# Swapped operand of the scores: second turn on TensorE, or a transfer from SBUF to SBUF

## Chip, cores and metric

One core of a Trainium2 chip. The time is the device time of the program in microseconds (us). Engines: TensorE (PE; its weight loads are PEld), VectorE (DVE), ScalarE (ACT), GpSimd (POOL), SyncE (SP), which issues all transfers of this kernel.

## What is computed

Attention that keeps 32 scores of each row, then two layers of expert networks. Cut to what matters:

```python
# q, k, v: (2, 8, 576, 64) float32; 2 batches, 8 heads
scores = (1 / sqrt(64)) * q @ k.transpose(0, 1, 3, 2)
kth = the 32nd largest score of each row
attn = softmax(where(scores >= kth, scores, -1e9))
x = (attn @ v) -> (1152, 512)
# 4 experts: out += p[:, e] * (relu(x @ w1[e]) @ w2[e]);  w1: (4, 512, 1024), w2: (4, 1024, 512)
# then a gated layer: ((x @ w_a) * (x @ w_b)) @ w_out;    w_a, w_b: (512, 1536), w_out: (1536, 512)
```

Which scores are kept depends on small differences, so most products are made nearly in float32.

## The kernel before

**Products.** Most operands are split into a high part, rounded to the fp32r format, and a low part, the rest. For the scores, k is turned so that its 64 high values and 64 low values of a row stand on 128 partitions, [high; low]. q is turned into two operands: [high; low], which gives high x high + low x low, and [low; high], which gives the two mixed products. The two matmuls add up in PSUM (`scores`, L765; `lh` counts the two operands).

**Tiles and groups.** The 1152 rows of q are nine tiles: eight of 128 rows, and one, MIX, with the last 64 rows of both batches. They are worked through in four groups of 1, 2, 3 and 3 tiles (`GROUPS`), MIX being the last tile of group 3. A group goes through four pairs of heads; `start_pair` (L679) prepares a pair: loads q (`qraws`), splits it (`split2`, L597), turns it and evicts it. Then each tile of the pair is a step: scores of both heads, their eviction (L794), four rounds of top-k on DVE (`MAX8` L815, `MATCH_REPLACE8` L823), mask and softmax on ACT and POOL (L846, L850, L854), scaling (L865), the turning of the probabilities (L538) and their product with v. When a group's four pairs are done, its experts' matmuls can run on PE between the steps of the next groups; the experts of group 3 and the gated layer stand behind the attention.

**Preparing q (L708 to L751).** Per head j, ACT writes the high part twice (blocks 0 and 2 of three) and DVE (first step) or POOL writes the low part in block 1. A turn then transposes blocks 0 and 1 and blocks 1 and 2 of each tile into one PSUM tile:

```python
                for i in range(T):
                    for lh in range(2):
                        tr(p[:, i, lh], sqv()[:, j, i, lh:lh + 2].rearrange("p a d -> p (a d)"), identr)
```

This is a turn of 2 T transposes per head, evicted by ACT into `qts` (L743, for the very first one by DVE, L739). For MIX the columns of each batch are copied into `qm` (L749), which holds zeros elsewhere; there is one `qm`, so its next contents wait for the last scores that read it (`qm_read`).

**PSUM.** `atts` are two double banks that take turns: scores, turns of k, q and probabilities all pass through them.

**Order.** Every operation is given to `Plan` with its engine, an estimated duration, a key (the lower, the sooner) and what it waits for. `best` simulates 42 orders, with transfers that land some time after their issue, and keeps the one with the lowest mean over three reruns. The engines then execute that order strictly, SP its transfers too (`load`, L514; all show as L517). All matmuls have line L535, all transposes L538.

Of the kernel before, what the change touches and what calls it, by code (L numbers as in the profile page):

```python
# [21 lines left out]
MIX = "mix"  # L22
# [354 lines left out]
def body(tc, q, k, v, probs, w1, w2, wa, wb, wo, out):  # L377
# [73 lines left out]
    qspls = big.slots("qspl", 1, 2 * 3 * 3 * D)  # L451
    qts = big.slots("qt", 2, 3 * 256)
# [100 lines left out]
    def last_rows(x, b):  # L553
        return x[b, :, MAIN:S].rearrange("h p d -> p h d")
# [123 lines left out]

    def start_pair(c, h2, n):  # L679
# [22 lines left out]
        sqv = lambda: sq.ap[:, 0:2 * T * 3 * D].rearrange("p (h t a d) -> p h t a d", h=2, t=T, a=3)  # L702
# [8 lines left out]
        sp = {0: [], 1: []}  # L711
        for j in range(2):
            sp[j] += split2(lambda j=j: sqv()[:, j, 0:m], lambda j=j: rqv()[:, j], m, key + 0.03 + (0.004 * j if n == 0 else 0), lds, [rq, sq], eng)
            if m < T:
                if not qrem_done:
                    for b in range(B):
                        qrem_done.append(load(lambda b=b: qrem[b * REM:(b + 1) * REM], lambda b=b: last_rows(q, b), key - 2, (), (), 131072, since=60e3))
                sp[j] += split2(lambda j=j: sqv()[:, j, m:T], lambda j=j: qrem[:, h + j].unsqueeze(1), 1, key + 0.03, qrem_done, [sq], eng)
        pair.q, pair.qd = {}, {}
        for j in range(2):  # L720
            at, qt = ms.tile() if n == 0 else atts.tile(key + 0.04), qts.tile(n)
            if n == 0:
                pv = lambda at=at: at.ap[:, 0:256].rearrange("p (t l n) -> p t l n", l=2, n=128)
            else:
                pv = lambda at=at: at.ap.rearrange("p b (t l n) -> p (b t) l n", l=2, n=128)

            def turn(j=j, pv=pv):
                p = pv().bitcast(F32R)
                for i in range(T):
                    for lh in range(2):  # L730
                        tr(p[:, i, lh], sqv()[:, j, i, lh:lh + 2].rearrange("p a d -> p (a d)"), identr)

            o = tensor(2 * T * TURN_R, turn, key + (0.025 if n == 0 and j == 0 else 0.04), sp[j] + [ready], [at, sq])
            qtv = lambda qt=qt: qt.ap.rearrange("p (t l n) -> p t l n", l=2, n=128)
            pair.q[j] = qt
            if n == 0 and j == 0:

# [728 lines left out]
```

## Time and profile before

| | |
|---|---|
| median of 3 runs | 829.12 us (829.0 to 829.53) |
| profiled execution | 828.9 us; its span, first to last instruction, 827.1 us |
| PE busy / DVE / ACT / POOL | 795.7 / 738.8 / 537.4 / 351.7 us |
| mean granted TensorE clock | 0.988 |
| moved by DMA | 129.68 MB, mean 157 GB/s |

Busy time is the time in which an engine has an instruction in work; matmuls overlap, so a busy PE is not one at its peak. A stretch of the span is read by the engine that is full in it and by what the others wait for there; idle time of an engine that nobody waits for costs nothing. The chain that ended last is followed back from the last instruction.

### The profile page before, as it was taken

What the parts mean: (1) busy time and instruction counts of PE and PEld (TensorE: products, weight loads), DVE (VectorE), ACT (ScalarE), POOL (GpSimd) and SP (SyncE); (2) the same over time, 40 slices, a digit from 0 to 9 for tenths busy, and PEclk for the clock granted to TensorE, in tenths of its full rate; (3) what the DMA queues carried; (4) which work ended last, traced back from release to release, by engine and by line L of the source; (5) the groups of instructions that cost most, each with busy time, mean ns of one, the idle gap of its engine ahead of it and who ended that gap; (6) DMA issues with size and microseconds to landing.
All of it is one profiled execution on the core that took longest, in us unless ns stands there. A gap on an engine that the chain in (4) does not pass through costs nothing.

```text
span 827.1 us, 14615 instructions
## 1 busy us (share of the span) xinstructions
PE 795.7 (96%) x5285; PEld 711.2 (86%) x5285; DVE 738.8 (89%) x1447; ACT 537.4 (65%) x953; POOL 351.7 (43%) x333
## 2 busy tenths in 40 slices
PE   7589999999999999999999999999999999999997
PEld 6477777798888789899989899989998989899996
DVE  7999999999899999999985899988867899997654
ACT  6878887999898989997765666766534633341110
POOL 3524333797978867755320201222213334432220
PEclk9789999999999999999999999999999999999999
DMA  6839976755466252433234646989320412221013
GB/s 218 257 102 339 310 230 218 235 166 176 155 195 200 81 193 85 159 103 103 77 128 159 205 146 220 331 269 324 112 94 4 151 52 103 76 78 52 1 52 114
DMA packets 91416, 129.68 MB, mean 157 GB/s; under 512 B 10832, under 2 KB 67152, under 8 KB 89808
## 3 DMA queue, kind: packets, MB, share of 16 engines
q1 hardware_dynamic: 91344, 128.75, 47.4%
q8 instruction: 41, 0.67, 0.3%
q14 instruction: 31, 0.25, 0.1%
HBM read 115.36 MB, written 13.37 MB: 156 GB/s over the span
## 4 chain that ended last, share of the span: by engine, by line
PE 65%; DVE 17%; ACT 10%; POOL 3%; issue 3%; DMA 1%; SPq 0%; POOLq 0%; DVEq 0%; ACTq 0%
PE ps L535 63%; DVE low L815 8%; DVE low L823 6%; PE ps L538 3%; POOL mid L981 2%; ACT mid L980 2%; ACT low L854 1%; ACT low L846 1%; ACT lowa L794 1%; ACT low L865 1%; ACT lowa L923 1%; DMA raw<-in_moe_w_dram 1%; POOL low L850 1%; ACT mid L1050 1%; DVE mid L1054 0%
## 5 line engine op out<-in xcount | busy, mean ns | idle before, releaser
L535 PE MATMUL ps<-mid 128*128 128x512 f32 x1092 | 278.7, 394 | 1.4 <-POOL mid L981 1.3
L535 PEld LDWEIGHTS ps<-mid 128*128 128x128 f32 x1092 | 198.6, 188 | 35.1 <-POOL mid L981 2.2
L535 PE MATMUL ps<-xs,mid 128*128 128x384 f32 (+1 forms) x1152 | 204.8, 321 | 2.6 <-DVE mid L1054 2.1
L535 PEld LDWEIGHTS ps<-xs,mid 128*128 128x128 f32 x1152 | 184.3, 189 | 11.9 <-DVE mid L1054 2.9
L815 DVE MAX8 low<-low 128x8 f32<-128x576 f32 x216 | 154.5, 748 | 0.1
L1271 POOL TENSOR_TENSOR low<-low 128x512 int32<-128x512 int32 x36 | 51.3, 1424 | 169.7 <-DVE low L1268 110.4
L981 POOL TENSOR_TENSOR mid<-raw,mid 128x1024 fp32r<-128x1024 f32 x48 | 115.0, 2409 | 7.4 <-ACT mid L980 5.5
L850 POOL TENSOR_TENSOR low<-lowa,low 128x576 f32<-128x576 f32 x70 | 99.2, 1438 | 36.6 <-ACT low L846 36.5
L980 ACT ACTIVATE mid<-raw 128x1024 fp32r<-128x1024 f32 x96 | 102.1, 1072 | 16.6 <-PE ps L535 12.0
L823 DVE MATCH_REPLACE8 low<-low 128x576 f32<-128x576 f32 x144 | 106.2, 743 | 0.0
L535 PE MATMUL ps<-xs,big 128*128 128x320 f32 (+1 forms) x576 | 87.7, 296 | 0.1
L535 PEld LDWEIGHTS ps<-xs,big 128*128 128x128 f32 x576 | 81.3, 190 | 2.5 <-DVE low L1360 0.3
L981 DVE TENSOR_TENSOR mid<-raw,mid 128x1024 fp32r<-128x1024 f32 x48 | 63.1, 1314 | 6.7 <-ACT mid L980 6.6
L535 PE MATMUL ps<-lowa_again,big 128*128 128x320 f32 (+1 forms) x432 | 67.0, 297 | 1.2 <-ACT rest L1369 0.8
L1050 ACT ACTIVATE mid<-ps 128x384 fp32r<-128x384 f32 (+1 forms) x96 | 44.3, 464 | 35.2 <-PE ps L535 32.5
L535 PEld LDWEIGHTS ps<-lowa_again,big 128*128 128x128 f32 x432 | 61.5, 189 | 3.8 <-ACT rest L1369 1.1
L865 ACT ACTIVATE low<-low 128x576 f32<-128x576 f32 x70 | 52.1, 790 | 16.3 <-DVE low L862 16.2
L538 PE MATMUL ps<-identr,low 128*128 128x128 f32 x360 | 52.5, 282 | 8.8 <-ACT low L865 7.8
L1054 DVE SCALAR_TENSOR_TENSOR mid<-ps,mid 128x384 fp32r<-128x384 f32 (+1 forms) x96 | 48.3, 505 | 12.7 <-ACT mid L1050 12.3
L846 ACT ACTIVATE low<-lowa,low 128x576 f32<-128x576 f32 x70 | 53.7, 786 | 7.3 <-POOL low L840 7.3
L538 PEld LDWEIGHTS ps<-identr,low 128*128 128x128 f32 x360 | 42.7, 144 | 17.8 <-ACT low L865 11.3
L794 ACT ACTIVATE lowa<-ps 128x576 f32<-128x576 f32 x72 | 47.4, 663 | 15.4 <-POOL low L850 11.3
(119 smaller groups left out, 1221.9 us busy)
## 6 DMA issues: line engine op xcount, KB each, us to landing
raw<-in_moe_w_dram SPq DMA_DIRECT2D x122, 512.0 KB, 4.0
big<-kscr SPq DMA_DIRECT2D x20, 576.0 KB, 5.4
low<-in_v_dram SPq DMA_DIRECT2D x24, 256.0 KB, 3.6
low<-in_moe_w_b_dram SPq DMA_DIRECT2D x12, 512.0 KB, 3.7
low<-in_moe_w_a_dram SPq DMA_DIRECT2D x12, 512.0 KB, 4.1
low<-in_moe_w_out_dram SPq DMA_DIRECT2D x12, 512.0 KB, 4.4
wscr<-big SPq DMA_DIRECT2D x6, 1024.0 KB, 7.1
mid<-wscr SPq DMA_DIRECT2D x6, 1024.0 KB, 4.8
```

Of the source, the lines that this page charges most:

```text
L535: nc.tensor.matmul(out, l, r, **kw)
L538: nc.tensor.transpose(out, a, i)
L794: S, lambda: nc.scalar.activation(s.ap.rearrange("p (c n) -> p c n", c=2), at.ap[:, :, 0:HALF], AF.Copy),
L815: 62 + 1.04 * width, lambda at=at, cs=cs: nc.vector.max(m8v()[:, x, cs], at()), key + 0.02 * r, [done],
L823: lambda at=at, cs=cs: nc.vector.match_replace(out=src[1](), in_to_replace=m8v()[:, x, cs], in_values=at(), imm_value=LOW),
L846: S, lambda x=x, s=s: nc.scalar.activation(ev(x), s.ap, AF.Relu, bias=endv()[:, x, 1:2], scale=-STEEP),
L850: pool_(S), lambda x=x, s=s: nc.gpsimd.tensor_tensor(ev(x), s.ap, ev(x), op=ALU.subtract), ks, [a], [s, ep]
L865: S, lambda x=x: nc.scalar.activation(ev(x), ev(x), AF.Copy, scale=sums.ap[:, x:x + 1]),
L980: hi = scalar(1024, lambda: nc.scalar.activation(u.ap[:, 0:1024], r.ap, AF.Copy), 500 + s, [ld], [u, r], sbuf=True)
L981: sub = lambda eng: eng.tensor_tensor(u.ap[:, 1024:2048], r.ap, u.ap[:, 0:1024], op=ALU.subtract)
L1050: n, lambda h=h, p=p: nc.scalar.activation(h.ap[:, 0:n], p.ap[:, 0:n], AF.Relu), -1000, [o], [h, p]
L1271: return gpsimd(pool_(512), lambda: nc.gpsimd.tensor_tensor(t().bitcast(I32), fold(c.ap.bitcast(I32)), fold(lowv().bitcast(I32)), op=ALU.a ...
```

## The change

Group 0 keeps its two turns per head (`first_queries`). In groups 1 to 3 (`queries`) q is split into a high and a low part once, for both heads in one instruction per engine; one turn for both heads makes [high; low] only, and one ACT instruction evicts it into `qa`. Two transfers then copy partitions 64 to 127 of `qa` to partitions 0 to 63 of `qb` and the other way round, which makes [low; high]. There are two `qa` and one `qb`. For MIX two ACT copies fill the first half of `qm`, and two transfers make the swapped half. A pair's scores wait for both transfers.

```diff
@@
     big.at = 2048
     kspls = big.slots("kspl", 1, 2 * M4 * 2 * D)
     bts = big.slots("bt", 4, 2 * S)
-    qspls = big.slots("qspl", 1, 2 * 3 * 3 * D)
-    qts = big.slots("qt", 2, 3 * 256)
+    qspls = big.slots("qspl", 1, 2 * 3 * 2 * D)
+    qas = big.slots("qa", 2, 2 * 3 * 128)
+    qbs = big.slots("qb", 1, 2 * 3 * 128)
@@
 
     qm_read = [[], []]
 
+    def first_queries(pair, n, key, eng, rqv, tiles, lds):
+
+        rq, sq = tiles
+        qa = qas.tile(n)
+        sqv = lambda: sq.ap[:, 0:2 * 3 * D].rearrange("p (h t a d) -> p h t a d", h=2, t=1, a=3)
+        pair.qd, pair.q = {}, [qa]
+        pair.qv = lambda j, i, lh: qa.ap[:, (2 * j + lh) * 128:(2 * j + lh + 1) * 128]
+        for j in range(2):
+            sp = split2(lambda j=j: sqv()[:, j], lambda j=j: rqv()[:, j], 1, key + 0.03 + (0.004 * j if n == 0 else 0), lds, tiles, eng)
+            at = ms.tile() if n == 0 else atts.tile(key + 0.04)
+            pv = (lambda at=at: at.ap[:, 0:256]) if n == 0 else (lambda at=at: at.ap[:, 0, 0:256])
+
+            def turn(j=j, pv=pv):
+                for lh in range(2):
+                    tr(pv().bitcast(F32R)[:, lh * 128:(lh + 1) * 128], sqv()[:, j, 0, lh:lh + 2].rearrange("p a d -> p (a d)"), identr)
+
+            o = tensor(2 * TURN_R, turn, key + (0.025 if n == 0 and j == 0 else 0.04), sp + [ready], [at, sq])
+            qv = lambda j=j: qa.ap[:, j * 256:(j + 1) * 256]
+            if n == 0 and j == 0:
+                pair.qd[j] = [vector(dve(256), lambda pv=pv, qv=qv: nc.vector.tensor_copy(qv(), pv()), -901.5, [o], [at, qa])]
+            else:
+                pair.qd[j] = [scalar(256, lambda pv=pv, qv=qv: nc.scalar.activation(qv(), pv(), AF.Copy), -901.5 + j, [o], [at, qa])]
+
+    def queries(pair, n, key, eng, rqv, tiles, lds):
+
+        rq, sq = tiles
+        T, h, m = pair.T, pair.h, len([t for t in pair.tiles if t != MIX])
+        qa, qb, at = qas.tile(n), qbs.tile(n), atts.tile(key + 0.04)
+        sqv = lambda: sq.ap[:, 0:2 * T * 2 * D].rearrange("p (h t a d) -> p h t a d", h=2, t=T, a=2)
+        sp = split(lambda: sqv()[:, :, 0:m, 0], lambda: sqv()[:, :, 0:m, 1], rqv, 2 * m * D, key + 0.03, lds, tiles, eng)
+        if m < T:
+            if not qrem_done:
+                for b in range(B):
+                    qrem_done.append(load(lambda b=b: qrem[b * REM:(b + 1) * REM], lambda b=b: last_rows(q, b), key - 2, (), (), 131072, since=60e3))
+            sp += split(lambda: sqv()[:, :, m, 0], lambda: sqv()[:, :, m, 1], lambda: qrem[:, h:h + 2], 2 * D, key + 0.03, qrem_done, [sq], eng)
+
+        def turn():
+            p = at.ap.bitcast(F32R)
+            for j in range(2):
+                for i in range(T):
+                    tr(p[:, j, i * 128:(i + 1) * 128], sqv()[:, j, i].rearrange("p a d -> p (a d)"), identr)
+
+        o = tensor(2 * T * TURN_R, turn, key + 0.04, sp + [ready], [at, sq])
+        w = m * 128
+        av = lambda: qa.ap[:, 0:2 * w].rearrange("p (j n) -> p j n", j=2)
+        bv = lambda: qb.ap[:, 0:2 * w].rearrange("p (j n) -> p j n", j=2)
+        e = scalar(2 * w, lambda: nc.scalar.activation(av(), at.ap[:, :, 0:w], AF.Copy), -901, [o], [at, qa])
+        got = [e] + [
+            load(lambda r=r: bv()[r * 64:(r + 1) * 64].bitcast(F32), lambda r=r: av()[(1 - r) * 64:(2 - r) * 64].bitcast(F32), -500, [e], [qa, qb], 512 * w)
+            for r in range(2)
+        ]
+        pair.qd, pair.q = {0: got, 1: got}, [qa, qb]
+        pair.qv = lambda j, i, lh: (bv() if lh else av())[:, j, i * 128:(i + 1) * 128]
+        if m < T:
+            es_ = [
+                scalar(
+                    2 * REM, lambda b=b: nc.scalar.activation(
+                        qm[:, :, b, 0, b * REM:(b + 1) * REM], at.ap[:, :, w + b * REM:w + (b + 1) * REM], AF.Copy
+                    ), -900, [o] + qm_read[0] + qm_read[1], [at],
+                ) for b in range(B)
+            ]
+            qm_read[:] = [], []
+            pair.md = es_ + [
+                load(lambda r=r: qm[r * 64:(r + 1) * 64, :, :, 1].bitcast(F32), lambda r=r: qm[(1 - r) * 64:(2 - r) * 64, :, :, 0].bitcast(F32), -400, es_, (), 1 << 17)
+                for r in range(2)
+            ]
+
     def start_pair(c, h2, n):
 
         pair = Pair()
@@
         m = len(norm)
         rq, sq = qraws.tile(key), qspls.tile(key)
         rqv = lambda: rq.ap[:, 0:2 * m * D].rearrange("p (h m d) -> p h m d", h=2, m=m)
-        sqv = lambda: sq.ap[:, 0:2 * T * 3 * D].rearrange("p (h t a d) -> p h t a d", h=2, t=T, a=3)
...
-        sp = {0: [], 1: []}
-        for j in range(2):
-            sp[j] += split2(lambda j=j: sqv()[:, j, 0:m], lambda j=j: rqv()[:, j], m, key + 0.03 + (0.004 * j if n == 0 else 0), lds, [rq, sq], eng)
-            if m < T:
-                if not qrem_done:
-                    for b in range(B):
-                        qrem_done.append(load(lambda b=b: qrem[b * REM:(b + 1) * REM], lambda b=b: last_rows(q, b), key - 2, (), (), 131072, since=60e3))
-                sp[j] += split2(lambda j=j: sqv()[:, j, m:T], lambda j=j: qrem[:, h + j].unsqueeze(1), 1, key + 0.03, qrem_done, [sq], eng)
-        pair.q, pair.qd = {}, {}
-        for j in range(2):
-            at, qt = ms.tile() if n == 0 else atts.tile(key + 0.04), qts.tile(n)
-            if n == 0:
-                pv = lambda at=at: at.ap[:, 0:256].rearrange("p (t l n) -> p t l n", l=2, n=128)
-            else:
-                pv = lambda at=at: at.ap.rearrange("p b (t l n) -> p (b t) l n", l=2, n=128)
-
-            def turn(j=j, pv=pv):
-                p = pv().bitcast(F32R)
-                for i in range(T):
-                    for lh in range(2):
-                        tr(p[:, i, lh], sqv()[:, j, i, lh:lh + 2].rearrange("p a d -> p (a d)"), identr)
-
-            o = tensor(2 * T * TURN_R, turn, key + (0.025 if n == 0 and j == 0 else 0.04), sp[j] + [ready], [at, sq])
-            qtv = lambda qt=qt: qt.ap.rearrange("p (t l n) -> p t l n", l=2, n=128)
-            pair.q[j] = qt
...
+        (first_queries if c == 0 else queries)(pair, n, key, eng, rqv, [rq, sq], lds)
         for b in batches(tiles):
             vt = vts.tile(n)
             pair.v[b] = vt
@@
         at, s = atts.tile(n - AHEAD), ss.tile(n)
         if t == MIX:
             bs = list(range(B))
-            after = pair.qd[j] + sum((pair.kd[b][j:j + 1] for b in bs), [])
+            after = pair.md + sum((pair.kd[b][j:j + 1] for b in bs), [])
             used = [pair.k[b] for b in bs]
         else:
             bs = [t[0]]
             after = pair.qd[j] + pair.kd[t[0]][j:j + 1]
-            used = [pair.k[t[0]], pair.q[j]]
+            used = [pair.k[t[0]]] + pair.q
 
         def emit():
             if t == MIX:
                 parts = [(qm[:, j, b], pair.k[b].ap[:, j * S:(j + 1) * S]) for b in bs]
             else:
-                parts = [(pair.q[j].ap.rearrange("p (t l n) -> p t l n", l=2, n=128)[:, i], pair.k[t[0]].ap[:, j * S:(j + 1) * S])]
+                parts = [(None, pair.k[t[0]].ap[:, j * S:(j + 1) * S])]
             for c in range(2):
                 for m_, (a, kt) in enumerate(parts):
                     for lh in range(2):
                         mm(
-                            at.ap[:, c, 0:HALF], a[:, lh], kt[:, c * HALF:(c + 1) * HALF],
+                            at.ap[:, c, 0:HALF], pair.qv(j, i, lh) if a is None else a[:, lh], kt[:, c * HALF:(c + 1) * HALF],
                             start=(m_ + lh == 0), stop=(m_ == len(parts) - 1 and lh == 1),
                         )
```

The lines of the changed kernel are moved by one up to L677: its matmuls are L536, its transposes L539, its transfers L518. The whole order is planned anew. Two places:

PE at the second pair of group 2, from the last scores of the pair before it (`big` is where k and q stand, `identr,big` a turn of q, `identr,low` a turn of probabilities, `raw,low` and `xs,mid` expert matmuls). Before:

```order
L535 MATMUL ps<-big 128x288 x4
L538 MATMUL ps<-identr,big 128x128 x6
L535 MATMUL ps<-raw,low 128x512
L538 MATMUL ps<-identr,big 128x128 x6
L535 MATMUL ps<-raw,low 128x512 x2
L535 MATMUL ps<-xs,mid 128x256 x3
L535 MATMUL ps<-raw,low 128x512
L538 MATMUL ps<-identr,low 128x128 x9
L535 MATMUL ps<-xs,mid 128x256 x6
L535 MATMUL ps<-big 128x288 x4
```

Changed:

```order
L536 MATMUL ps<-big 128x288 x4
L539 MATMUL ps<-identr,big 128x128 x6
L536 MATMUL ps<-raw,low 128x512 x3
L536 MATMUL ps<-xs,mid 128x256 x3
L536 MATMUL ps<-raw,low 128x512
L539 MATMUL ps<-identr,low 128x128 x9
L536 MATMUL ps<-xs,mid 128x256 x6
L536 MATMUL ps<-big 128x288 x8
```

The second turn is gone; the three 128x512 matmuls that stood around it now follow the one turn directly, and the pair's scores (the last row) come after the same expert matmuls and probability turns as before.

SP at the third pair of group 2 (`big<-kscr` reloads k, `raw<-in_moe_w` loads expert weights, `big<-big` are the two new transfers). Before:

```order
L517 DMA low<-in_v_dram 128x2x256 x2
L517 DMA big<-kscr 128x1152
L517 DMA raw<-in_moe_w_dram 128x4x256
L517 DMA big<-kscr 128x1152
L517 DMA low<-in_q_dram 128x2x128
L517 DMA raw<-in_moe_w_dram 128x2x512 x2
L517 DMA raw<-in_moe_w_dram 128x4x256 x2
```

Changed:

```order
L518 DMA low<-in_v_dram 128x2x256 x2
L518 DMA big<-kscr 128x1152
L518 DMA raw<-in_moe_w_dram 128x2x512
L518 DMA big<-big 64x768 x2
L518 DMA low<-in_q_dram 128x2x128
L518 DMA raw<-in_moe_w_dram 128x4x256
L518 DMA big<-kscr 128x1152
```

The two transfers of `q` stand behind a weight load, whose buffer POOL frees, and ahead of the next pair's q load and of a reload of k.

## Rows read from the trace of the kernel before

**Rows 1.** Busy time (and instructions) by stretch; last: clock, DMA share, GB/s.

```profile
core 0: us, PE busy (x) PEld busy (x) DVE busy (x) ACT busy (x) POOL busy (x), PEclk, DMA share, GB/s
0.00:60.00 60.00, 43.81 (x286) 36.70 (x287) 54.43 (x122) 44.71 (x92) 22.74 (x42) 0.86 0.59 189
...
60.00:345.00 285.00, 276.04 (x2081) 237.23 (x2079) 279.47 (x602) 251.81 (x472) 193.98 (x174) 1.00 0.61 199
...
345.00:820.00 475.00, 473.45 (x2914) 435.68 (x2913) 402.83 (x722) 240.83 (x391) 134.94 (x118) 1.00 0.38 128
```

**Rows 2.** Chain that ended last, page and pieces: start us, us, what.

```profile
PE 65%; DVE 17%; ACT 10%; POOL 3%; issue 3%; DMA 1%; SPq 0%; POOLq 0%; DVEq 0%; ACTq 0%
...
667.01 155.38 PE ps L535 x972
```

**Rows 3.** PE's waits: us, times, longest; first row whole span, others 60 to 345 us.

```profile
PE ps L538 <- ACT low L865: 7.8, 6, 2.4
...
PE ps L535 <- ACT low L1229: 2.3, 3, 1.2
PE ps L538 <- ACT low L865: 2.1, 2, 1.9
PE ps L538 <- ACT lowa L794: 0.4, 1, 0.4
PE ps L535 <- ACT lowa L923: 0.2, 1, 0.2
```

**Rows 4.** Timeline of PE, two stretches: start us, us, what.

```profile
97.59 0.53 PE L538 MATMUL ps<-identr,big 128*128 128x128 f32 x4 [0.37 <-ACT lowa L794]
98.08 1.98 PE L535 MATMUL ps<-low 128*128 128x512 f32 x4
...
149.11 0.63 PE L538 MATMUL ps<-identr,big 128*128 128x128 f32 x6
149.58 1.09 PE L535 MATMUL ps<-raw,low 128*128 128x512 f32 x2
150.49 0.68 PE L538 MATMUL ps<-identr,big 128*128 128x128 f32 x6
151.00 1.95 PE L535 MATMUL ps<-raw,low 128*128 128x512 f32 x4
...
155.70 0.76 PE L535 MATMUL ps<-big 128*128 128x288 f32 x4
```

**Rows 5.** ACT on q: busy, mean; last three rows 60 to 345 us.

```profile
L743 ACT ACTIVATE big<-ps 128x512 fp32r<-128x512 f32 x16 | 9.4, 604 | 0.2 <-PE ps L538 0.2
L743 ACT ACTIVATE big<-ps 128x768 fp32r<-128x768 f32 x8 | 6.5, 810 | 0.0
L600 ACT ACTIVATE big<-low 128x256 fp32r<-128x256 f32 x16 | 6.9, 445 | 0.0
...
L600 ACT ACTIVATE big<-low 128x384 fp32r<-128x384 f32 x8 | 3.8, 543 | 0.0
L600 ACT ACTIVATE big<-rest 128x128 fp32r<-128x128 f32 x8 | 2.9, 364 | 0.0
L749 ACT ACTIVATE qm<-ps 128x128 fp32r<-128x128 f32 x12 | 2.7, 311 | 0.0
```

**Rows 6.** Timelines of ACT and of SP: an eviction of q, an issue.

```profile
150.50 0.82 ACT L743 ACTIVATE big<-ps 128x768 fp32r<-128x768 f32 x1
...
187.08 0.34 SPq L517 DMA_DIRECT2D big<-kscr  x1
```

**Rows 7.** Issue to landing (last column), 100 to 160, then 160 to 370.

```profile
low<-in_q_dram SPq DMA_DIRECT2D x3, 128.0 KB, 5.4
...
raw<-in_moe_w_dram SPq DMA_DIRECT2D x43, 512.0 KB, 3.7
low<-in_q_dram SPq DMA_DIRECT2D x4, 128.0 KB, 2.3
```

**Rows 8.** Two groups of expert matmuls, whole span: busy us, mean ns.

```profile
L535 PE MATMUL ps<-mid 128*128 128x512 f32 x1092 | 278.7, 394 | 1.4 <-POOL mid L981 1.3
...
L535 PE MATMUL ps<-raw,low 128*128 128x512 f32 x56 | 29.4, 610 | 2.3 <-ACT low L1229 2.3
```

**Rows 9.** SP's waits, 60 to 345 us: us, times, longest.

```profile
SPq L517 <- PE ps L535: 77.9, 41, 6.1
SPq L517 <- POOL mid L981: 53.9, 22, 4.7
```

**Rows 10.** Issue to landing, 55 to 130 us: 128 and 64 partitions.

```profile
low<-in_q_dram SPq DMA_DIRECT2D x4, 128.0 KB, 5.0
rest<-in_q_dram SPq DMA_DIRECT2D x2, 128.0 KB, 6.3
```

More of the change, by code (lines that the diff above doesn't have):

```diff
@@ L719, in start_pair @@
-        pair.q, pair.qd = {}, {}
-        for j in range(2):
-            at, qt = ms.tile() if n == 0 else atts.tile(key + 0.04), qts.tile(n)
-            if n == 0:
-                pv = lambda at=at: at.ap[:, 0:256].rearrange("p (t l n) -> p t l n", l=2, n=128)
-            else:
-                pv = lambda at=at: at.ap.rearrange("p b (t l n) -> p (b t) l n", l=2, n=128)
-            def turn(j=j, pv=pv):
-                p = pv().bitcast(F32R)
-                for i in range(T):
-                    for lh in range(2):
-                        tr(p[:, i, lh], sqv()[:, j, i, lh:lh + 2].rearrange("p a d -> p (a d)"), identr)
-            o = tensor(2 * T * TURN_R, turn, key + (0.025 if n == 0 and j == 0 else 0.04), sp[j] + [ready], [at, sq])
-            qtv = lambda qt=qt: qt.ap.rearrange("p (t l n) -> p t l n", l=2, n=128)
-            pair.q[j] = qt
-            if n == 0 and j == 0:
-                pair.qd[j] = [vector(
-                    dve(256), lambda pv=pv, qtv=qtv: nc.vector.tensor_copy(qtv()[:, 0:m], pv()[:, 0:m]), -901.5, [o], [at, qt]
-                )]
-            else:
-                pair.qd[j] = [scalar(
-                    m * 256, lambda pv=pv, qtv=qtv: nc.scalar.activation(qtv()[:, 0:m], pv()[:, 0:m], AF.Copy), -901.5 + j, [o], [at, qt]
-                )]
-            if m < T:
-                for b in range(B):
-                    cs = slice(b * REM, (b + 1) * REM)
-                    pair.qd[j].append(scalar(
-                        128, lambda j=j, b=b, cs=cs, pv=pv: nc.scalar.activation(qm[:, j, b, :, cs], pv()[:, m, :, cs], AF.Copy),
-                        -900, [o] + qm_read[j], [at],
-                    ))
```

## Prediction, made before the changed kernel ran

> **What bounds the kernel now.** I read the busy time by stretch first, then the chain that ended last, then PE's own waits, then single turns on PE's timeline. From 60 to 345 us DVE is busy 279.5 of 285 us and PE 276.0; from 345 to 820 us PE is busy 473.5 of 475 us and DVE 402.8 [rows 1]. The first stretch is the attention, whose top-k fills DVE while PE fits expert matmuls around it; in the second, PE alone sets the end, and the chain that ended last has 65% of its length on PE, its last piece 155.4 us of matmuls without a break [rows 2]. So a microsecond of PE work taken out of the attention is worth a microsecond at the end if PE fills the hole with expert matmuls that now stand after 345 us; there is such work, since PE has no gap for 475 us. PE's whole loss from 60 to 345 us is 285 - 276 = 9 us, of which its waits for ACT are 2.3 + 2.1 + 0.4 + 0.2 = 5.0 us (L1229 is an eviction of group 0's experts, L865 the scaling of the probabilities) [rows 3].
>
> **What goes.** Each of the 12 pairs of groups 1 to 3 has two turns now, one per head, of 4 (group 1) or 6 transposes; it keeps one of the same length. The order shows exactly 64 transposes fewer on PE and nothing else gone there. On the timeline a turn of 6 holds PE from 149.11 to 149.58 us and again from 150.49 to 151.00, 0.47 and 0.51 us; one of 4 from 97.59 to 98.08, 0.49 us [rows 4]. That is 4 x 0.49 + 8 x 0.46 to 0.51. I take 0.47 for the eight: 2.0 + 3.7 = **5.7 us of PE**, all in the stretch where PE runs at 97%. None of it is covered by other work: where PE is the bound, it is on the path.
>
> ACT loses half of the evictions (9.4/2 + 6.5/2 = 8.0 us), half of the splits (6.9/2 + 3.8/2 + 2.9/2 = 6.8 us) and 8 of 16 copies into qm (8 x 0.311 = 2.5 us), 17.3 us in all [rows 5]; POOL has 16 instructions fewer and the same elements. I cost this at nothing, neither gain nor loss: ACT is busy 251.8 of 285 us [rows 1] and not the bound. If it is worth something, it is through PE's waits for ACT; bounds 0 to all 5.0 us of them, -5.0 us [rows 3]. DVE's instruction count is unchanged.
>
> **What comes.** 24 transfers of 128 or 192 KB from SBUF to SBUF, two per pair, and 8 of 128 KB for qm, together 4.7 MB beside the 199 GB/s x 285 us = 57 MB that the kernel moves from 60 to 345 us at a DMA share of 0.61 [rows 1]: 8% more, and room for it. What matters is that the scores of a pair now wait for: turn, eviction, two issues on SP, landing. For the second pair of group 2 the parts can be read: its first turn starts at 149.11 us, its eviction at 150.50 and lasts 0.82; an issue of SP takes 0.34, twice [rows 6]. A landing is not shown for such a transfer. The nearest rows are the 128 KB loads of q: 5.4 us from issue to landing between 100 and 160 us, where the DMA engines are crowded, and 2.3 us from 160 us on [rows 7]. So the swapped operand is there 1.39 + 0.82 + 0.34 + (2.3 to 5.4) = 4.9 to 8.0 us after the turn starts. The room: that pair's first scores start at 155.70 [rows 4], 6.6 us after the turn, 6.1 without the second turn's 0.51. Short by 0 to 1.9 us; I take 1.0, as the place lies in the crowded stretch.
>
> Of the other pairs, the last has least between turn and scores by the changed order: 15 matmuls of 512 columns (278.7/1092 = 0.255 us each), 3 expert matmuls of 384 columns and 9 transposes, 4.6 us or more [rows 8]. It needs 4.9 - 0.5 = 4.4 us after the turn, the low landing being the right one there: 0. The first pair's room holds only 13 matmuls, but its transposes wait for the softmax: of the 7.8 us that PE loses to L865, 5.7 lie before 60 us [rows 3], so PE stands there in any case; 0. The nine others have 20 to 72 matmuls in between; the tightest three of them, in the crowded half, have about 8.2 to 8.5 us (one: four fp32 matmuls of 512 columns at 2 x 29.4/56 = 1.05 us and sixteen small ones), against 7.5 at most [rows 8]: 0.
>
> Behind a late operand stand, on PE, the pair's remaining scores and the expert matmuls after them; on SP, the next q load, weight loads and a reload of k. SP is walked in order, so a swap that waits for ACT's eviction holds those. They wait anyway: SP's queue stood 77.9 us for PE and 53.9 us for POOL's weight splits from 60 to 345 us [rows 9], and loads run ahead of their use. Cost 0 for that. A swap can also stand behind a load that itself waits; that is the second rival.
>
> **The sum.** 828.9 us (profiled) - 5.7 + 1.0 = 824.2. The profiled execution lies 0.2 under the median 829.12, so against the runs **824.4 us**.
>
> **One rule weighed.** The transfers use 64 partitions each, one per direction. The only like rows are two 128 KB loads into 64 partitions, 6.3 us to land, beside 5.0 us for 128 KB over 128 partitions in the same stretch [rows 10]: 1.3 us longer, with different neighbours. The Trainium skill, page "SBUF — State Buffer", sections "Door 1: The DMA port swizzle" and "Can I just issue two DMAs to hit both halves?", says that 64 partitions reach only half of the ports and that two such transfers run one after the other; the trace agrees in direction only. What half the rate would do here is the third rival.
>
> **The rivals.**
>
> 1. *More than PE's share (0.14).* ACT's 17.3 us come out of the softmax chain, and PE's waits for L865 and L794 shrink as well. For it: ACT is at 88% in that stretch and more than half of PE's loss is for it [rows 1, 3]. Against: DVE at 98% sets the pace of the steps, and nothing of L1229 changes. Time: 829.1 - 5.7 - 5.0 = 818.4 at most; 820 to 822 if half comes.
>
> 2. *Slower: the swap is stuck on SP's queue (0.11).* The order puts a weight load that waits for POOL directly before the swap of group 2's third pair, and a load waiting for PE before others. SP's waits for POOL average 53.9/22 = 2.5 us [rows 9]. If the swap is held that long at every pair, 7.5 + 2.5 = 10.0 us are needed after the turn in the crowded half and 4.4 + 2.5 = 6.9 later: the second pair of group 2 is short by 1.9 + 2.5 = 4.4, the three tight ones by 1.8, 1.8 and 1.5, the last by 2.3, 11.8 us. Time: 829.1 - 5.7 + 11.8 = 835.2. It decides once the shortfalls pass 5.7 us, half of this. Against: the written order comes from a plan with a landing time in it, and SP waits of that length stand where nothing is urgent.
>
> 3. *No gain: half rate for half the partitions (0.10).* By rows, 512 KB land in 3.7 us and 128 KB in 2.3 from 160 us on [rows 7], so 384 KB (both transfers) cost 1.4 us of moving; at half the rate 2.8, that is 1.4 us later at every pair. The second pair of group 2 is then short by up to 1.9 + 1.4 = 3.3, the last by 1.0, the three tight ones by some 0.6 each: 6.1 us against 5.7, time 829.5.
>
> 4. *No gain: PE's hole stays empty (0.17).* DVE sets the pace until 345 us, and the expert matmuls that could move forward lack their split weights, so PE idles 5.7 us more: 829.1. For it: PE already idles 9 us there. Against: a hole is 0.47 us per pair and closes by sliding the static order; 17 us of ACT are free for more splits.
>
> That the change does not do what it says is out: the order shows the 64 transposes gone and the 32 transfers there.
>
> **How the numbers follow.** Forecast 0.48, rivals 0.14, 0.11, 0.10, 0.17. The whole order of every engine is planned anew, so the places of small waits change everywhere; that widens the forecast by some 2 us to either side, 822 to 827. A measurement of this kernel can tell about 0.2% (1.7 us) from no change. Faster by more than that (below 827.5): forecast 0.46 and rival 1's 0.14, with 0.02 from the edge of rival 4, 0.62. Same: rival 4's 0.14, half of rival 3, 0.02 of the forecast, 0.21. Slower (above 830.8): rival 2's 0.11, the other half of rival 3 and 0.01 of rival 4, 0.17. The range 820 to 831.5 leaves out most of rival 2 above and the far end of rival 1 below.
>
> **What would show it.** Right: transposes from big 64 fewer at about 0.08 us each, PE's busy time from 60 to 345 us about the same and the stretch after it 5 us shorter; PE waiting for a DMA into big about 1 us in all; SBUF transfers landing in 2.3 to 5.4 us. Wrong: PE waiting for DMA into big or qm for more than 5 us (rivals 2 and 3, told apart by whether the issue or the landing is late); PE's idle time before 345 us up by the 5.7 us (rival 4) or down (rival 1); DVE's first MAX8 of a step waiting for L794 far above its present few us.

## The result, and the profile after

The changed kernel takes **820.28 us** (median of 4 runs, 820.14 to 821.03) beside 829.06 us (4 runs) for the kernel before on the same chip: ratio **0.9901, 95% interval 0.9888 to 0.9913**, 8.8 us or 1.0% faster. The forecast was 824.4, the range 820.0 to 831.5. The sign was right and the time lies just inside the range; the experiments show that three terms of the sum behind it were wrong. The profiled execution of the changed kernel is 820.39 us, its span 818.6, so 8.5 us of span are to be accounted for. Up to L677 a line of the kernel before has a number one higher; the scaling of the probabilities (L865) is L892, the score eviction (L794) L821, the weight splits (L980, L981) L1007 and L1008, the top-k's MAX8 (L815) L842, the experts' evictions and their splits (L1050, L1054) L1077 and L1081.

Busy time by stretch, with the columns of [rows 1]:

```profile
0.00:60.00 60.00, 44.09 (x282) 36.19 (x283) 54.18 (x121) 44.56 (x91) 23.69 (x42) 0.97 0.63 198
60.00:345.00 285.00, 277.13 (x2068) 238.90 (x2067) 283.17 (x612) 245.63 (x445) 197.05 (x162) 1.00 0.70 216
345.00:820.00 475.00, 467.84 (x2875) 429.88 (x2873) 397.91 (x716) 234.79 (x382) 130.00 (x115) 1.00 0.39 128
```

In the attention PE and DVE are a little fuller than before, ACT is 6.2 us emptier, and the DMA share rises from 0.61 to 0.70; PE's work after 345 us is 5.6 us less. By PE's account of the whole span, the 8.5 us are 6.6 us less busy time (795.7 to 789.1) and 1.9 us less idle time (31.4 to 29.5). Where the time went shows best with the span cut at the end of the last MAX8, the end of the top-k: 425.69 + 0.76 us in the kernel before, 426.13 + 0.75 in the changed one.

```profile
0.00:426.50 426.50, 401.09 (x2950) 348.82 (x2951) 415.39 (x884) 360.25 (x673) 252.34 (x245) 0.98 0.55 179
426.50:827.10 400.60, 394.59 (x2337) 362.43 (x2335) 323.39 (x564) 177.10 (x281) 99.31 (x88) 1.00 0.40 133
```

The same cut in the changed kernel:

```profile
0.00:426.90 426.90, 403.12 (x2926) 349.98 (x2927) 418.95 (x889) 350.13 (x640) 249.70 (x229) 1.00 0.62 192
426.90:818.60 391.70, 385.94 (x2296) 355.00 (x2295) 316.31 (x558) 174.85 (x277) 101.05 (x88) 1.00 0.40 134
```

The top-k ends at the same time, 0.4 us later. Behind it the kernel before has 400.6 us with 2337 matmuls, the changed one 391.7 us with 2296. So **the front is no shorter; 41 expert matmuls, some 9 us, have moved from behind the top-k to in front of it**. In front, 64 transposes are gone and the same some 40 matmuls have come (2950 to 2926; a few records can be missing).

PE's waits from 60 to 345 us (total, times, longest), the answer to [rows 3]:

```profile
PE ps L536 <- DMA big<-big: 2.9, 3, 1.3
PE ps L539 <- ACT low L892: 1.7, 2, 1.1
PE ps L536 <- ACT low L1256: 1.4, 2, 0.7
```

The waits for the swapped operand are new, 2.9 us. The longest is at the second pair of group 2, the place that the prediction named; the two others, 1.12 us at the second pair of group 1 and 0.47 us at the third of group 3, the sum had at 0. PE's timeline at the named place, as in [rows 4]:

```profile
148.34 0.63 PE L539 MATMUL ps<-identr,big 128*128 128x128 f32 x6
...
154.63 0.29 PE L536 MATMUL ps<-big 128*128 128x288 f32 x1
156.20 1.17 PE L536 MATMUL ps<-big 128*128 128x288 f32 x7 [1.28 <-DMA big<-big]
```

The first score reads the unswapped operand and runs; the second stands 1.28 us and starts 7.9 us after the turn, at the upper end of the 4.9 to 8.0 us forecast. The issues and landings (median in the last column) from 160 to 370 us, beside the second part of [rows 7]:

```profile
raw<-in_moe_w_dram SPq DMA_DIRECT2D x44, 512.0 KB, 3.5
...
big<-big SPq DMA_DIRECT2D x8, 128.0 KB, 6.8
qm<-qm SPq DMA_DIRECT2D x8, 128.0 KB, 5.7
big<-big SPq DMA_DIRECT2D x4, 192.0 KB, 5.5
low<-in_q_dram SPq DMA_DIRECT2D x4, 128.0 KB, 4.3
```

These medians, 5.5 to 6.8 us, lie above the forecast's 2.3 to 5.4. The single transfers differ by their place. At the second pair of group 2 the two swaps took 4.6 and 5.0 us, inside the forecast; over the 32 transfers the landings go from 2.3 to 8.5 us. The quick ones are those of the first pair (2.3 and 2.6) and of the last; this is the view from 360 to 372 us:

```profile
big<-big SPq DMA_DIRECT2D x2, 128.0 KB, 2.3
qm<-qm SPq DMA_DIRECT2D x2, 128.0 KB, 2.5
```

The q loads take 4.3 us from 160 to 370 us, 2.0 more than before. ACT's work on q is halved as forecast, the evictions for instance (groups 1 to 3, beside [rows 5]):

```profile
L726 ACT ACTIVATE big<-ps 128x512 fp32r<-128x512 f32 x8 | 4.8, 595 | 0.0
...
L726 ACT ACTIVATE big<-ps 128x768 fp32r<-128x768 f32 x4 | 3.2, 806 | 0.0
```

By such groups the evictions, splits and copies lost 7.9 + 6.8 + 2.0 = 16.7 us, near the 17.3 forecast. ACT's busy time over the span fell by less, from 537.4 to 525.0 us: neighbouring instructions overlap (the durations of the kernel before add up to 623.0 us), so a group's sum counts more than the engine gains.

### The profile page after: what moved, and what is told of

Read it like the earlier page. It is cut to its first block, busy times and chain, and to the rows that moved or that the text cites. A ratio compares the mean times of both kernels' runs of the same rounds, so it can differ in the third digit from the quotient of the medians.

```text
span 818.6 us, 14468 instructions
## 1 busy us (share of the span) xinstructions
PE 789.1 (96%) x5221; PEld 705.0 (86%) x5221; DVE 735.3 (90%) x1447; ACT 525.0 (64%) x917; POOL 350.7 (43%) x317
## 4 chain that ended last, share of the span: by engine, by line
PE 64%; DVE 26%; ACT 4%; DMA 3%; issue 1%; POOL 1%; SPq 0%; POOLq 0%; ACTq 0%
PE ps L536 61%; DVE low L842 12%; DVE low L850 10%; PE ps L539 2%; DMA raw<-in_moe_w_dram 1%; DVE mid L1081 1%; DMA big<-big 1%; DVE low L1106 1%; DMA low<-in_k_dram 1%; ACT low L892 1%; ACT mid L1007 0%; ACT lowa L821 0%; ACT low L881 0%; DVE rest L1387 0%; POOL low L877 0%
## 5 line engine op out<-in xcount | busy, mean ns | idle before, releaser
L536 PE MATMUL ps<-mid 128*128 128x512 f32 x1092 | 278.4, 394 | 0.0
L536 PEld LDWEIGHTS ps<-mid 128*128 128x128 f32 x1092 | 198.5, 188 | 32.8 <-DVE mid L1081 0.7
L536 PE MATMUL ps<-xs,mid 128*128 128x384 f32 (+1 forms) x1152 | 204.3, 321 | 1.2 <-DVE mid L1081 1.1
L536 PEld LDWEIGHTS ps<-xs,mid 128*128 128x128 f32 x1152 | 185.0, 189 | 9.9 <-DVE mid L1081 2.2
L842 DVE MAX8 low<-low 128x8 f32<-128x576 f32 x216 | 155.0, 749 | 0.1
L1008 POOL TENSOR_TENSOR mid<-raw,mid 128x1024 fp32r<-128x1024 f32 x48 | 115.2, 2406 | 8.0 <-ACT mid L1007 6.9
L1007 ACT ACTIVATE mid<-raw 128x1024 fp32r<-128x1024 f32 x96 | 101.7, 1063 | 17.7 <-PE ps L536 16.5
L536 PE MATMUL ps<-xs,big 128*128 128x320 f32 (+1 forms) x576 | 87.8, 297 | 0.1
L536 PEld LDWEIGHTS ps<-xs,big 128*128 128x128 f32 x576 | 81.3, 190 | 2.5 <-DVE low L1387 0.3
L536 PE MATMUL ps<-lowa_again,big 128*128 128x320 f32 (+1 forms) x432 | 66.8, 297 | 1.0 <-ACT rest L1396 0.8
L536 PEld LDWEIGHTS ps<-lowa_again,big 128*128 128x128 f32 x432 | 61.5, 190 | 3.4 <-ACT rest L1396 1.1
L1008 DVE TENSOR_TENSOR mid<-raw,mid 128x1024 fp32r<-128x1024 f32 x48 | 58.9, 1229 | 6.0 <-ACT mid L1007 5.7
L1077 ACT ACTIVATE mid<-ps 128x384 fp32r<-128x384 f32 (+1 forms) x96 | 43.3, 456 | 30.4 <-PE ps L536 27.8
L892 ACT ACTIVATE low<-low 128x576 f32<-128x576 f32 x70 | 51.1, 773 | 16.3 <-DVE low L889 16.1
L539 PE MATMUL ps<-identr,low 128*128 128x128 f32 x360 | 53.4, 283 | 7.3 <-ACT low L892 6.6
L539 PEld LDWEIGHTS ps<-identr,low 128*128 128x128 f32 x360 | 42.3, 144 | 19.2 <-ACT low L892 13.4
L1081 DVE SCALAR_TENSOR_TENSOR mid<-ps,mid 128x384 fp32r<-128x384 f32 (+1 forms) x96 | 48.2, 506 | 11.3 <-ACT mid L1077 10.8
L881 ACT ACTIVATE low<-low 128x576 f32<-128x576 f32 x70 | 54.6, 781 | 3.1 <-POOL low L877 3.1
```

What stands on the lines that cost most here:

```text
L536: nc.tensor.matmul(out, l, r, **kw)
L539: nc.tensor.transpose(out, a, i)
L842: 62 + 1.04 * width, lambda at=at, cs=cs: nc.vector.max(m8v()[:, x, cs], at()), key + 0.02 * r, [done],
L881: lambda x=x: nc.scalar.activation(ev(x), ev(x), AF.Exp, bias=endv()[:, x, 0:1], scale=scale, accum_out=sums.ap[:, x:x + 1]),
L892: S, lambda x=x: nc.scalar.activation(ev(x), ev(x), AF.Copy, scale=sums.ap[:, x:x + 1]),
L1007: hi = scalar(1024, lambda: nc.scalar.activation(u.ap[:, 0:1024], r.ap, AF.Copy), 500 + s, [ld], [u, r], sbuf=True)
```

## The experiments

Twelve runs in three groups, each with runs of the kernel before on the same chip (828.56, 828.23 and 827.93 us). Every ratio is against the runs of the same chip. What a run with the changed kernel's order is worth is read as the difference of its ratio from 0.9901; the gains of kernels with an order of their own are differences of medians. Seven of the twelve (x_before_half, x_nowait, x_noswap, y_act, y_both, r_act, r_pe) leave products out or use an operand in place of another; they are there for their time alone. The theories (A, B and so on) are those of the text that stands ahead of each result.

### One load put back or taken out, the order kept

**x_turns**, the changed kernel with its turns made twice:

```
-            for j in range(2):
+            for j in 2 * list(range(2)):
```

> After's order, with each turn of groups 1 to 3 made twice into the same place: the 64 transposes are back on PE, and nothing else changes (one eviction, the swaps stay). The changed kernel takes 820.3 us. Theory A (PE is the bound through the attention, and the turns are paid in full, 4 x 0.49 + 8 x 0.47 = 5.7 us): 825.5 to 826.0. Theory B (much of the gain of 8.8 us is not the turns: ACT's relief, or the newly planned order): 820.5 to 823.5, PE's waits down by what the total does not show.

Measured 823.71 us, ratio 0.9938 (0.9922 to 0.9955): 0.0037 or 3.1 us over the changed kernel. PE's busy time rose from 789.1 to 793.0 us: 64 transposes are 3.9 us of PE, not 5.7. The time is just above theory B's 823.5 and well below theory A: the turns are paid in part, and they don't explain 8.8 us.

**x_before_half**, the kernel before without the second turns:

```
-                    for lh in range(2):
+                    for lh in range(2 if c == 0 else 1):
```

> The kernel before, its order kept, with the second turn of every pair of groups 1 to 3 left out of PE (64 transposes); its eviction, splits and copies stay on ACT and copy what lies in the tile, so the products that use the second order are not the reference's. Theory A (the turns are 5.7 us of PE, and the rest of the gain comes with the order or with ACT): 829.1 - 5.7 = 823.4, about 3 us above the changed kernel. Theory B (turns are worth little by themselves, since DVE's top-k paces the attention): 826 to 829. If it comes out at 820 to 821, the turns alone are the whole gain and all else of the change cancels.

Measured 828.01 us, ratio 0.9997 (0.9987 to 1.0006): no difference from zero. PE's busy time fell from 795.7 to 791.6 us, the span by 1.3 only; PE's idle time rose from 31.4 to 34.2 us. The hole stayed empty, as theory B has it.

**x_nowait**, the changed kernel whose scores don't read the swapped operand:

```
-        pair.qv = lambda j, i, lh: (bv() if lh else av())[:, j, i * 128:(i + 1) * 128]
+        pair.qv = lambda j, i, lh: av()[:, j, i * 128:(i + 1) * 128]
...
-    ... pair.qv(j, i, lh) if a is None else a[:, lh], ...
+    ... pair.qv(j, i, lh) if a is None else a[:, 0], ...
```

> The changed kernel with its order and its transfers kept, but the scores of groups 1 to 3 read the unswapped operand for both products, so no matmul waits for a swap; the products of exchanged halves are left out of the result in this way. PE waits 2.9 us for swaps in the changed kernel's profile (3 waits). Theory A (those waits are on the path like all of PE's): 820.3 - 2.9 = 817.4. Theory B (a late swap only takes the place of another wait, since DVE sets the pace of the steps): 819.5 to 820.5, with PE's waits for ACT or DVE up by as much.

Measured 820.04 us, ratio 0.9897 (0.9880 to 0.9914): the 2.9 us of waits are worth 0.3 us at most likely, not told from zero. PE's idle time did not fall (817.6 - 787.8 = 29.8 us, 29.5 in the changed kernel). Over its whole span PE waits instead for the scores' eviction and for DVE's splits:

```profile
PE ps L539 <- ACT lowa L821: 4.3, 3, 3.1
...
PE ps L536 <- DVE mid L1081: 2.2, 3, 1.6
```

In the changed kernel they are 2.9 us and 1.1. This is what theory B says.

**x_act**, the changed kernel with ACT's work on q doubled (evictions, copies into qm, high halves):

```
-        e = scalar(2 * w, lambda: nc.scalar.activation(av(), at.ap[:, :, 0:w], AF.Copy), -901, [o], [at, qa])
+        e = scalar(2 * w, lambda: [nc.scalar.activation(av(), at.ap[:, :, 0:w], AF.Copy) for _ in range(2)], -901, [o], [at, qa])
...
```

The copies and the high halves are changed in the same way.

> The changed kernel with its order kept; ACT makes each eviction and each copy into qm of groups 1 to 3, and the high half of each split of q, twice into the same place: roughly the 17 us of ACT that the change took away are back (evictions 8.0, splits' high halves 5.3, copies 2.5). The swaps stand behind the second eviction, so they start up to 0.8 us later. Theory A (ACT's relief is worth nothing, as costed): 820.3, up to 821.5 for the later swaps. Theory B (rival 1, the relief is what carried the gain past the turns' 5.7 us): 823 to 825, with PE's waits for the probabilities' scaling and for the evictions up.

Measured 830.12 us, ratio 1.0018 (1.0008 to 1.0027): 9.7 us over the changed kernel, more than either theory allowed. It put 17.1 us of busy time on ACT (525.0 to 542.1), more than the 12.4 that the change took off. The swaps are not the cause: PE waits for them 0.4 us. PE's waits over the whole span:

```profile
PE ps L539 <- ACT low L892: 14.4, 11, 2.2
```

In the changed kernel this row is 6.6 us in 5. And DVE, whose share of the experts' work needs ACT's evictions first, waits from 60 to 430 us:

```profile
DVE mid L1081 <- ACT mid L1077: 6.7, 8, 1.7
```

against 0.6 us. So the written order of the changed kernel needs ACT's relief, above all for the scaling of the probabilities. Whether the relief by itself gives the gain, this run can't say.

### The relief in the old order

**y_act** leaves the second head's eviction, high half and copies out of ACT in the kernel before (PE's order stays the same, instruction by instruction):

```
+                    m * 256, lambda j=j, pv=pv, qtv=qtv: c and j or nc.scalar.activation(qtv()[:, 0:m], pv()[:, 0:m], AF.Copy), ...
+                        128, lambda j=j, b=b, cs=cs, pv=pv: j or nc.scalar.activation(...
+            m * 2 * D, lambda: high or nc.scalar.activation(dst()[:, :, ::2], ...
```

> The kernel before in its own order, PE as before (both turns of every pair), but ACT no longer makes the second head's eviction, its high half and its copies into qm in groups 1 to 3, half of ACT's work on q there (about 17 us of ACT less, as in the changed kernel). The second head's products use the first head's operand, so they are not the reference's. Theory R (what the first four runs suggest: the relief of ACT carries the gain, the turns count for little while ACT is loaded): 822 to 825, as with the changed kernel plus its turns (823.7). Theory O (the gain comes from the newly drawn order and the two loads do little in the old one): 827 to 829. Theory A (the turns carry it): 828 to 829.

Measured 828.59 us, ratio 1.0006 (0.9997 to 1.0016): no gain. Theory R, in the form it had, fell.

**y_both** leaves the second turns out as well:

```
-                    for lh in range(2):
+                    for lh in range(1 if c else 2):
```

> The run just described with the second turn of each pair left out of PE too, 64 transposes fewer: the kernel before in its own order with both savings of the change and none of its transfers; the second head's products use the first head's operand, so they are not the reference's. Theory R, with the turns worth their 5.7 us or most of it once ACT is relieved: 819 to 821, no more than 1 us from the changed kernel's 820.3. Theory O: 824 to 828. The swaps and the new order then cost or bring what lies between this run and the changed kernel.

Measured 827.41 us, ratio 0.9993 (0.9983 to 1.0002). Both savings together, without one transfer, bring 0.6 us by the ratios in the old order, as theory O has it. The last MAX8 says why:

```profile
423.28 0.75 DVE L817 MAX8 low<-low 128x8 f32<-128x576 f32 x1
```

The span is 825.4 us, so 825.4 - 424.0 = 401.4 us lie behind the end of the top-k. For all runs, some of them described below, from the same rows:

| kernel | order | end of top-k | span behind it |
|---|---|---|---|
| before | old | 426.5 | 400.6 |
| x_before_half | old | 425.2 | 400.6 |
| y_act | old | 424.5 | 401.1 |
| y_both | old | 424.0 | 401.4 |
| after | new | 426.9 | 391.7 |
| x_turns | new | 428.9 | 391.7 |
| x_nowait | new | 425.9 | 391.7 |
| x_noswap | new | 428.0 | 391.7 |
| x_act | new | 436.4 | 391.8 |
| b_seed1 (before) | its own | 419.5 | 405.9 |
| a_seed1 (after) | its own | 431.2 | 391.5 |
| a_seed7 (after) | its own | 426.5 | 391.8 |
| r_act | its own | 429.4 | 389.8 |
| r_pe | its own | 422.4 | 401.7 |

Each engine walks a fixed order. What stands behind the last top-k step there stays behind it, so the part behind is one number per order, within 0.8 us, whatever is saved in front. A saving in front can only bring the end of the top-k forward; DVE, busy 279.5 of the 285 us from 60 to 345, lets it come 2.5 us sooner for 4 us of PE and 11 of ACT (y_both). Getting more needs another order. Another order alone trades one part for the other: b_seed1, the same work as before, ends its top-k 7.0 us sooner and has 5.3 us more behind it. So only the sum of the two parts tells what a kernel is worth.

**x_noswap**, x_nowait with the 32 transfers dropped:

```
-            load(lambda r=r: bv()[r * 64:(r + 1) * 64].bitcast(F32), ...
+            plan.add("SP", 0, lambda: None, -500, [e], [qa, qb], nbytes=512 * w)
```

> The changed kernel with its order, without the 32 transfers, and the scores of groups 1 to 3 reading the unswapped operand for both products (the products of exchanged halves are left out). Against the run that kept the transfers but did not wait for them (820.0): what the transfers cost by their traffic and their places on SP's queue. Theory free (DMA share 0.70 leaves room): 819.5 to 820.5. Theory crowding (loads behind them land 2 us later): 817 to 819.

Measured 821.02 us, ratio 0.9911 (0.9894 to 0.9928): no faster than with the transfers. Their traffic and their places on SP's queue cost nothing that can be told.

### The load and the order together

**r_act**: the kernel before relieved on ACT as in y_act, PE's turns kept, but the left-out instructions are not in the plan either, so the order is planned for that load (its lines have numbers up to three higher than those of the kernel before):

```
-        a = scalar(
+        a = first[0] if high else scalar(
...
+            if c and j:
+                pair.q[1], pair.qd[1] = pair.q[0], pair.qd[0]
+                continue
```

> The kernel before with ACT relieved (no eviction, no high half and no copy into qm for the second head of groups 1 to 3, about 17 us of ACT less) and PE's turns kept, and this time the order of all engines planned for that load. The second head's products use the first head's operand, so they are not the reference's. In the old order the same relief brought nothing (828.6). Theory R2 (ACT's relief carries the gain, but only through an order that is planned with it): 820 to 823. Theory P2 (what the new order uses is the 5.7 us of PE): 827 to 830. An order's luck is some 2 us to either side.

Measured **821.52 us, ratio 0.9919** (0.9904 to 0.9933): 6.4 us, with every turn still on PE, as theory R2 has it.

**r_pe**: the kernel before without the second turns, planned for it, ACT's work kept:

```
-            o = tensor(2 * T * TURN_R, turn, ...
+            o = tensor((1 if c else 2) * T * TURN_R, turn, ...
```

> The kernel before with the second turn of each pair of groups 1 to 3 left out of PE (64 transposes) and ACT's work kept, the order planned for that load; the evictions copy what lies in the tile, so the products of the second order are not the reference's. In the old order this brought 0.5 us. Theory P2 (the turns are worth their 5.7 us once the order is planned for it): 822.5 to 825.5. Theory R2 (while ACT is loaded, PE waits instead): 826 to 829.

Measured 825.45 us, ratio 0.9966 (0.9954 to 0.9978): 2.5 us. It just meets the upper end of theory P2's range, and is well short of its 5.7.

How far the experts' work has come by 400 us tells the two apart. PE's two large groups of expert matmuls up to 400 us (busy, mean ns), kernel before:

```profile
L535 PE MATMUL ps<-xs,mid 128*128 128x256 f32 (+1 forms) x577 | 96.4, 306 | 2.6 <-DVE mid L1054 2.1 <-DVE low L1079 0.3
L535 PE MATMUL ps<-mid 128*128 128x512 f32 x327 | 87.4, 398 | 1.4 <-POOL mid L981 1.3
```

The same in r_act:

```profile
L535 PE MATMUL ps<-xs,mid 128*128 128x256 f32 (+1 forms) x611 | 101.6, 307 | 1.4 <-DVE mid L1057 1.0 <-DVE xs L1189 0.3
L535 PE MATMUL ps<-mid 128*128 128x512 f32 x336 | 89.2, 397 | 0.0
```

in the changed kernel:

```profile
L536 PE MATMUL ps<-xs,mid 128*128 128x256 f32 (+1 forms) x611 | 101.7, 307 | 1.2 <-DVE mid L1081 1.1
L536 PE MATMUL ps<-mid 128*128 128x512 f32 x336 | 89.7, 397 | 0.0
```

and in r_pe:

```profile
L535 PE MATMUL ps<-xs,mid 128*128 128x256 f32 (+1 forms) x582 | 94.0, 306 | 2.2 <-POOL mid L981 1.7 <-DVE mid L1054 0.5
L535 PE MATMUL ps<-mid 128*128 128x512 f32 x336 | 91.1, 401 | 2.0 <-POOL mid L981 1.3 <-DVE mid L1054 0.4 <-DVE xs L1186 0.3
```

r_act and the changed kernel stand at 611 + 336, 43 matmuls ahead of the kernel before; r_pe at 582 + 336, 14 ahead, with PE waiting 1.7 + 1.3 = 3.0 us for POOL's weight splits. Those splits begin on ACT. Up to 400 us, kernel before:

```profile
L980 ACT ACTIVATE mid<-raw 128x1024 fp32r<-128x1024 f32 x50 | 53.5, 1086 | 2.4 <-PE ps L535 1.7 <-DMA raw<-in_moe_w_dram 0.6
```

r_act:

```profile
L983 ACT ACTIVATE mid<-raw 128x1024 fp32r<-128x1024 f32 x53 | 56.0, 1067 | 2.5 <-PE ps L535 2.5
```

There are 53 in the changed kernel too, 51 in r_pe. So in r_act three more weight tiles are split by 400 us, PE's idle time falls to 25.7 us (819.1 - 793.4, before 31.4), and the part behind the top-k shrinks by 10.8 us while the top-k ends 2.9 later.

That the splits are what lets the matmuls come forward is read from these counts; no run changes the splits alone, and x_act has 52 of them by 400 us and only 915 matmuls of these two groups. Nor is ACT's time the only thing that r_act frees: a turn whose eviction is left out also gives its PSUM bank back sooner, and only one of two `qts` buffers is used per pair. No run separates these.

### How much is the luck of an order

**b_seed1**, **a_seed1** and **a_seed7** are the kernel before, and twice the changed kernel, with another series of drawn delays in the planner (1000, 1000 and 7000; 7000 was picked from eight by the planner's own rating):

```
-            draw = random.Random(r)
+            draw = random.Random(r + 1000)
```

> The kernel before with another series of drawn delays in the planner, the same as for the changed kernel's other order (824.4): the same work in another order. If the orders are all of one worth, 829 within 2 us. If the first order of before was an unlucky one and the change's 8.8 us are mostly luck, 823 to 826.

> The changed kernel with another series of drawn delays in the planner, so another order of the same work on every engine. It tells how much of the difference of 8.8 us may be the luck of the order: theory R says the order matters by 2 us or less (818.5 to 822.5), theory O by 4 us or more.

> The changed kernel with a third series of drawn delays, the one of eight whose order the planner itself rates best, by 1 us. If the changed kernel's order of 820.3 is typical: 818 to 822; if it was a lucky one and 824.4 is typical: 823 to 826. Under 819.5 it would be the better version of the two kernels.

Measured: before 827.26 us, ratio 0.9990 (0.9981 to 1.0000); changed 824.38 us, 0.9951 (0.9936 to 0.9966), and 821.43 us, 0.9921 (0.9904 to 0.9937). All three orders of the changed kernel have 391.5 to 391.8 us behind the top-k; they differ in its end (431.2 us in the slow one, 426.5 in the other). The order of b_seed1 is within the 2 us that its text allows; a_seed1 is as far off as theory O says (4.1 us), a_seed7 as near as a typical order should be. So the change is worth 3.9 to 8.8 us by the order drawn, some 6 on the mean of three against two of before, and the one that was timed is the best of three, which is luck. No run of the whole computation was faster.

The main finding does not hang on r_act's one order. Four orders were planned with ACT relieved: that of the changed kernel (after, x_turns, x_nowait, x_noswap), those of a_seed1 and a_seed7, and that of r_act. Run with this relief they have ratios from 0.9897 to 0.9951. Three orders were planned with ACT's full load (before, b_seed1, r_pe); their ratios are 0.9966 to 1. By 400 us the seven runs of the first kind have 52 or 53 weight splits on ACT and 930 to 955 matmuls of the two groups, the three of the second kind 50 or 51 and 904 to 918. The two of the seven that keep the 64 transposes (x_turns 0.9938, r_act 0.9919) lie among those that don't, so what the transposes are worth is not told apart from the luck of an order here.

## Why the prediction came out, and where its steps failed

**The signs.** The first signs that the prediction named for being right came: 64 transposes fewer, PE's busy time before 345 us much the same, and 5.6 us less of it after. They could not tell its explanation from another: r_act, with every turn kept, has 5.1 us less after 345 us too (468.3 against 473.5).

**The PE term, -5.7 us: wrong in size and in worth.** By PE's busy time the 64 transposes are 3.9 us (x_turns), 4.1 (x_before_half) and 4.3 (y_act to y_both), not 5.7. The likely reason is that a turn taken from one start to the next on the timeline counts work that overlaps its neighbours. And the step "None of it is covered by other work: where PE is the bound, it is on the path" failed: taken out of the old order the turns are worth 0.3 us (x_before_half) to 1.1 (y_both beside y_act), with an order planned for it 2.5, and put back into the new order 3.1. PE was at 97% in the attention, but a hole there is filled only if the order brings work forward, and that work has to be ready: r_pe's waits for POOL's splits, 3.0 us against 1.3 in the kernel before, point to the splits.

**ACT at nothing, "neither gain nor loss": the step that failed most.** The amount was about right, the worth was not. The reason given, ACT is busy 251.8 of 285 us and not the bound, holds for a fixed order only (y_act: no gain). Planned with it, the relief alone brings 6.4 us (r_act). Its bound of -5.0 us, all of PE's waits for ACT, was the wrong place to look: PE's waits for L865 and L794 in the whole span fell from 11.9 us to 9.5, and they are 8.6 in b_seed1, whose ACT has its full load. What the relief buys is expert matmuls in front of the top-k's end; most likely it does so by weight splits that are made in time.

**The swap, +1.0 us: the right place and mechanism, the wrong size and worth.** PE stands 2.9 us in three waits, 1.28 of them at the second pair of group 2, where 1.0 was forecast. Two places that the sum had at 0 make up the rest. At most other pairs the landing was mis-sized, with medians of 5.5 to 6.8 us from 160 to 370 us against 2.3 to 5.4; at the last pair the low landing of 2.3 held. In time it is worth 0.3 us or nothing (x_nowait), since other waits take its place.

**SP's queue at 0:** this held (x_noswap).

**The rivals.** The first, more than PE's share, came nearest: "820 to 822 if half comes"; it had 0.14, and its mechanism, shrinking waits of PE, covers 2.4 us. The fourth, the hole stays empty because the matmuls that could fill it lack their split weights, has the outcome of the old order, where the order itself keeps them back, and in part of r_pe. The forecast's answer to it, "17 us of ACT are free for more splits", names what most likely made the gain, but only as a remark. The second and third did not come: landings were late, but nobody waited for long. On the third, from 160 to 370 us the q loads land in 4.3 us with 128 KB over 128 partitions, the swaps of 128 KB in 5.7 to 6.8. The Trainium skill, page "SBUF — State Buffer", section "Can I just issue two DMAs to hit both halves?", says that two half-partition transfers are served one after the other. The medians agree in direction; but the last pair's swaps land in 2.3 and 2.5 us, as a q load did before [rows 7], so nothing of it shows where little else moves, and no run here separates it from the crowding elsewhere.

**The range.** "The whole order of every engine is planned anew" was allowed 2 us to either side; three orders of the changed kernel span 4.1. The forecast of 824.4 is just the time of the slowest of them (824.38), which is luck. Its errors went both ways: 2.6 to 3.2 us too much gain for PE (5.7 against 3.1 and 2.5), 6.4 too little for ACT, 0.7 to 1.0 too much cost for the wait. Put right, the sum gives 8.6 to 9.5 us, beside the 8.8 measured; the terms come from different orders, so this is no more than a rough agreement.

What is not settled: the 6.4 and the 2.5 us rest on one order each, and an order's luck is about as large as the smaller one. By which of the things that ACT's relief frees the matmuls come forward is argued, not shown.

## What to carry to other kernels

Where every engine walks a written order, ask first which phase paces the kernel and what work the order puts behind its end: the time is the sum of the two, and a saving in front shows only if the order can pull work forward. Then ask what that work needs; the engine that prepares it (here ACT, which begins the weight splits) can be worth more than the engine that looks full, though PE's waits for it are short. And before a change below one per cent is put down to its mechanism, time two or three orders of the same work.

## What was not expected of the hardware

- The landing of one and the same form of transfer, SBUF to SBUF over 64 partitions and 128 KB, goes from 2.3 us (the first and last pair) to 8.5 us (the third pair of group 3). From 160 to 370 us its medians, 6.8 and 5.7 us, are above the 4.3 of a load of the same size and the 3.5 of a 512 KB weight load; whether that comes from the form or from its place right behind others was not tested.
- Issuing such a transfer takes SP longer than issuing a reload of k. Two issues in a row at the second pair of group 2, on SP's timeline:

```profile
148.53 0.34 SPq L518 DMA_DIRECT2D big<-kscr  x1
150.60 1.11 SPq L518 DMA_DIRECT2D big<-big  x2
```

The two swaps take 0.56 us each on the mean, beside 0.34 for a reload of k. Over all 32 transfers the median is 0.60 us, that of the 20 reloads 0.34.
